# Quartered scores with full tables in the first two batches of a fused sliding-window attention and feed-forward kernel

## Chip, cores and metric

The kernel runs on one core of a Trainium2 chip. The metric is device microseconds of that core for one execution. A core has five engines with a queue of instructions each, worked off in order: TensorE (PE; weight loads are shown apart as PEld), VectorE (DVE), ScalarE (ACT), GpSimd (POOL) and SyncE (SP). [...] SyncE, ScalarE and GpSimd issue DMAs.

## The reference

Attention with a sliding window of 128 positions and a linear bias per head, then a feed-forward layer with a hard swish. The input is float32; the kernel computes in bf16 with float32 sums.

```python
B, H, S, D = 8, 8, 576, 64           # q, k, v: (B, H, S, D)
scores = q @ k.T / sqrt(D)
rel = pos[:, None] - pos[None, :]     # query position - key position
slopes = 2.0 ** (-8.0 * (arange(H) + 1) / H)
scores = where((rel >= 0) & (rel < 128), scores - slopes * abs(rel), -1e9)
x = softmax(scores) @ v               # -> (B*S, H*D) = (4608, 512)
h = x @ w_in                          # (4608, 2048)
out = (h * clip(h + 3, 0, 6) / 6) @ w_out   # (4608, 512), float32
```

## The kernel before

**Attention.** The work is cut into 32 pairs of heads, `g = 4 * batch + hp`, each with 576 positions in four key tiles of 128 and one of 64. Scores stand transposed in PSUM, keys on partitions and queries along the columns. A key tile j meets two blocks of queries: its own ("diagonal", rel from 0) and the next ("off", rel up to 127). Two PSUM buffers `score[0]` and `score[1]`, each of two banks (one bank per head of the pair), are handed out in turn by `score_banks()`.

Mask and bias reach the scores in two ways. In batches 2 to 7, `scores` works on quarters of TensorE's array (64 x 64: head e selects the rows, half of the key tile the columns), the exponential (`exp_diag`, `exp_off`) takes the bias as a column per partition (`bias_d`, `bias_o`), and GpSimd masks the result with `affine_select`. In batch 0 a table (`tab`, slopes times rel, with -2^30 where masked) is added in PSUM first: `tables_diag` and `tables_off` multiply it by the identity, `scores_diag` and `scores_off` add the products of k and q with 64 x 128 of the array, and one exponential of 1024 columns follows for each block. In batch 1 the off block has a table and the diagonal has bias columns and GpSimd's masks. `attend` (a whole pair in a score buffer), `attend_split` and `values` (in parts of three and two query tiles, in banks "av", "o" or "h") multiply by v, which has a column of ones, and VectorE divides by that column's result. `back` transposes a pair's result into `xT`, the input of the feed-forward part: by TensorE up to batch 1 and for two pairs of batch 2, by a transposing DMA afterwards.

**Loading.** q and k of batches 0 to 3 (k) or 2 (q) arrive as float32 in `ldbuf`, are cast to bf16 (`prepare`, `prepare_double`, `prepare_halves`) and transposed by TensorE: `transposes` for one pair on quarters of the array, `double...` and `wide...` for two pairs at once on the whole array. v is cast by `cast_v` or `cast_tokens`. The first 512 columns of w_in come as float32 through SyncE (`load_raw`, `cast_raw`), the rest of w_in and w_out through casting DMAs that GpSimd issues (`load_w_in`, `load_w_out`). Until w_out is loaded, `w_out_sb` holds the exponentials of batch 0 (`rooms`); those of batch 1 stand in `gbuf[1]`.

**Feed-forward.** Nine tiles of 512 tokens. `moe_up(nt, ms)` makes one of 16 column tiles: four matmuls of 512 columns into a PSUM bank, a ReLU on ScalarE (scaled by 1/6, bias 0.5), and on VectorE min with 1 times h into `gbuf`. `moe_down` does four of the 16 matmuls of an output tile per step. The up tiles use the two banks "h" in turn; `UP_BANKS` sends some of tile 0 to "av" and "o". `units` is the fixed list of these steps, and `fill(n)` takes the next n of them where their input exists (`done`).

**Order.** Everything is under a manual schedule: each engine's instructions stand in the order in which the Python calls them. `first_batch()` and `second_batch()` are written out by hand, with `fill` between the steps of attention; from pair 8 on `segment` does the same in a loop. `memset(ldbuf[2][:, 0:1])` near the end of `second_batch` (L768) is a fence: v of batch 2 is loaded into that buffer only after GpSimd has come to it. `warm_up(n)` runs n matmuls whose result nobody reads.

Of the kernel before, what the change touches and what calls it, by code (L numbers as in the profile page):

```python
# [10 lines left out]
FP32 = mybir.dt.float32  # L11
# [7 lines left out]
def kernel(  # L19
# [39 lines left out]
    tab = perm.tile([128, H, 2, 128], BF16)  # L59
# [63 lines left out]

    def constants():
        make_identity(nc, ident)
        nc.vector.memset(bias3, 0.5)
        nc.vector.memset(warm, 0.0)
        nc.scalar.activation(out=warm, in_=warm, func=ACT.Exp)
        nc.gpsimd.iota(rel_i, pattern=[[0, 1]], base=0, channel_multiplier=1)
        base = rpool.tile([128, NT], FP32, tag="r6", name="base")  # L130
        base_i = base[:, 0:256].bitcast(INT32).rearrange("p (s c) -> p s c", s=2)
        base_b = base[:, 256:384].bitcast(BF16).rearrange("p (s c) -> p s c", s=2)
        nc.gpsimd.iota(base_i, pattern=[[128, 2], [0, 128]], base=-192, channel_multiplier=1)
        nc.gpsimd.tensor_copy(out=base_b, in_=base_i)
        biases()
        nc.gpsimd.affine_select(out=base_b[:, 1, :], in_=base_b[:, 1, :], pattern=[[1, 128]],
                                channel_multiplier=-1, base=0,
                                compare_op=ALU.is_ge, fill=-(2.0 ** 30))
        nc.gpsimd.affine_select(out=base_b[:, 0, :], in_=base_b[:, 0, :], pattern=[[-1, 128]],
                                channel_multiplier=1, base=-1,  # L140
                                compare_op=ALU.is_ge, fill=-(2.0 ** 30))
        nc.vector.memset(kTb[0][:, :, 4, LAST:128], 0.0)
        for h in range(H):
            nc.vector.tensor_scalar(out=tab[:, h, :, :], in0=base_b, scalar1=slopes[h] / scale,
                                    scalar2=0.0, op0=ALU.mult, op1=ALU.add)
# [5 lines left out]
    def memsets_later():  # L151
        for i in range(2):
            nc.gpsimd.memset(p4buf[i], 1.0)
        nc.gpsimd.memset(kTb[1][:, :, 4, LAST:128], 0.0)
        nc.gpsimd.memset(vbuf[1][:, :, :, D:W], 1.0)
        nc.gpsimd.memset(vbuf[1][64:128, 4, :, 0:D], 0.0)
        nc.gpsimd.memset(tbuf[64:128, :, 4, :], 0.0)
# [7 lines left out]
    def biases():  # L165
        nc.vector.tensor_copy(out=rel_f, in_=rel_i)
        for h in range(H):
            nc.vector.tensor_scalar(out=bias_o[:, h:h + 1], in0=rel_f, scalar1=-192.0,
                                    scalar2=slopes[h], op0=ALU.add, op1=ALU.mult)

        for h in range(H):
            nc.vector.tensor_scalar(out=bias_d[:, h:h + 1], in0=rel_f, scalar1=-64.0,
                                    scalar2=slopes[h], op0=ALU.add, op1=ALU.mult)
# [20 lines left out]
    def second_w_in():  # L194
        nc.gpsimd.memset(w_out_sb[:, 4, 0:1], 0.0)
# [34 lines left out]
    def transposes(g, copies):  # L230
        b, hp = divmod(g, NP)
        for nm, dst, copy in (("q", qTb[b % 2], copies[0]), ("k", kTb[b % 2], copies[1])):
            src = st.pop((g, nm))
            tp = ps_h.tile([128, RT, RP], BF16, tag="h", name="tp", padded_shape=[128, 16, 64])
            for t in range(RT):
                for e in range(2):
                    r = slice(e * D, (e + 1) * D)
                    nc.tensor.transpose(tp[r, t, :], src[r, ts(t, D)], ident[r, r])  # L238
            copy(out=dst[:, hp, :, :].rearrange("p j c -> p (j c)")[:, 0:S].rearrange(
                "p (a t) -> p a t", t=RT), in_=tp.rearrange("p t a -> p a t"))  # L240
# [72 lines left out]
    def diag_tabled(g):  # L313
        return g < NP

    def tables_diag(g):
        scd = score_banks()
        st[g, "scd"] = scd
        for e in range(2 if diag_tabled(g) else 0):
            t = tab[:, 2 * (g % NP) + e, 1:2, :]  # L320
            nc.tensor.matmul(scd[:, e, :].rearrange("p (j c) -> p j c", j=4), lhsT=ident,
                             rhs=t.to_broadcast([128, 4, 128]), start=True, stop=False)

    def rooms(g):
        b, hp = divmod(g, NP)
        if full(g):
            room = w_out_sb if b == 0 else gbuf[1]
            for i, nm in enumerate(("pd", "po")):
                st[g, nm] = room[:, ds(4 * hp + 2 * i, 2), :].rearrange(
                    "p e (j c) -> p e j c", j=4)  # L330
        else:
            st[g, "pd"] = ppool.tile([128, 2, 4, 128], BF16, tag="pd", name="pd")
            st[g, "po"] = ppool.tile([128, 2, 4, 128], BF16, tag="po", name="po")

    def scores_diag(g):
        rooms(g)
        b, hp = divmod(g, NP)
        qT, kT = qTb[b % 2][:, hp, :, :], kTb[b % 2][:, hp, :, :]
        first = not diag_tabled(g)
        if (g, "scd") not in st:  # L340
            tables_diag(g)
        scd = st[g, "scd"]
        for j in range(4):
            for e in range(2):
                r = slice(e * D, (e + 1) * D)
                nc.tensor.matmul(scd[:, e, ts(j, 128)], lhsT=kT[r, j, :],  # L346
# [540 lines left out]
```

## Time and profile before

| | |
|---|---|
| timed runs | 320.58, 319.79, 320.45 us; median 320.45 us |
| profiled execution | span 317.9 us from first to last instruction; the profile lists no other time of it |
| instructions in it | 6980 |
| busy | PE 307.0 us, PEld 163.4, DVE 176.1, ACT 196.8, POOL 138.9 |
| granted TensorE clock | 1.000 of full |
| DMA | 52.43 MB, mean 165 GB/s |

A busy PE is not PE at its peak: matmuls are pipelined, and each row's duration holds some 0.17 us in which the next is already running. The distance between starts tells the rate. Rows of the timeline merge equal instructions (x4 is four of them) and give in brackets how long the engine was idle before, and what ended that.

### The profile page before, as it was taken

Reading aid. Unit: us, or ns where it says so; the run is one execution under the profiler, and the core shown is the slowest. Engines: PE = TensorE matmul, PEld = TensorE weight load, DVE = VectorE, ACT = ScalarE, POOL = GpSimd, SP = SyncE. Lnnn points to the kernel's source line nnn. Section 1 sums busy time; section 2 is a strip of 40 time slices with the busy share of each in tenths; the row PEclk is TensorE's granted clock in tenths of the full one; section 3 lists DMA queues with packets and bytes.
Section 4 is the critical chain, followed back from the end, with each engine's and each line's share of the span. In section 5 each row is a group of like instructions: output and inputs, shape, how many; then the busy total and the mean of one; then the engine's idle time right before and its main releaser. Section 6 shows DMA issues by size and latency. Waiting matters only on the chain.

```text
span 317.9 us, 6980 instructions
## 1 busy us (share of the span) xinstructions
PE 307.0 (97%) x2671; PEld 163.4 (51%) x2710; DVE 176.1 (55%) x344; ACT 196.8 (62%) x338; POOL 138.9 (44%) x247
## 2 busy tenths in 40 slices
PE   8889999999999999999999999999999999999996
PEld 3565474455554445555676644454444444444443
DVE  6677676554456654566465546564656455455510
ACT  3869986877767666766667756675764244244401
POOL 7358192674594684548463854472231000000000
PEclk9999999999999999999999999999999999999999
DMA  7999999999999999999999999934112100000112
GB/s 271 264 373 215 255 236 200 236 235 198 216 265 180 222 215 212 213 196 253 186 178 219 190 206 198 228 95 57 49 29 75 66 34 33 35 33 33 66 57 77
DMA packets 131425, 52.43 MB, mean 165 GB/s; under 512 B 118976, under 2 KB 122816, under 8 KB 131392
## 3 DMA queue, kind: packets, MB, share of 16 engines
q1 hardware_dynamic: 125648, 46.15, 69.0%
q0 software_dynamic: 3696, 3.67, 7.1%
q10 hardware_dynamic: 2048, 2.16, 2.2%
q8 instruction: 21, 0.34, 0.5%
q14 instruction: 12, 0.10, 0.1%
HBM read 36.70 MB, written 9.44 MB: 145 GB/s over the span
## 4 chain that ended last, share of the span: by engine, by line
PE 90%; ACT 3%; DVE 3%; issue 2%; POOL 0%; DVEq 0%; POOLq 0%; ACTq 0%
PE hps L532 38%; PE ops L587 37%; PE score L399 3%; PE av L463 2%; PE av L455 2%; DVE avs L485 1%; PE ops L568 1%; PE w L163 1%; ACT w_out_sb L422 1%; PE score L346 1%; PE tp L269 1%; ACT r L556 1%; DVE gbuf L557 1%; PE score L301 1%; PE score L357 1%
## 5 line engine op out<-in xcount | busy, mean ns | idle before, releaser
L556 ACT ACTIVATE r<-hps,bias 128x512 f32<-128x512 f32 x144 | 98.9, 689 | 84.2 <-PE hps L532 83.9
L557 DVE SCALAR_TENSOR_TENSOR gbuf<-r,hps 128x512 bf16<-128x512 f32 x144 | 98.8, 688 | 91.6 <-ACT r L556 90.1
L532 PE MATMUL hps<-xT,w_in_sb 128*128 128x512 bf16 (+1 forms) x623 | 142.0, 358 | 1.7 <-ACT xT L519 0.3
L587 PE MATMUL ops<-w_out_sb,gbuf 128*128 128x512 bf16 x538 | 133.8, 379 | 2.3 <-issue 1.8
L532 PEld LDWEIGHTS <-w_in_sb 128*128 128x128 bf16 x640 | 59.2, 98 | 54.0 <-issue 1.5
L587 PEld LDWEIGHTS <-gbuf 128*128 128x128 bf16 x560 | 52.4, 98 | 57.5
L427 POOL TENSOR_SCALAR_AFFINE_SELECT pd<-pd 128x512 bf16<-128x512 bf16 x48 | 29.4, 631 | 35.2 <-ACT pd L425 35.2
L436 POOL TENSOR_SCALAR_AFFINE_SELECT po<-po 128x512 bf16<-128x512 bf16 x48 | 30.1, 633 | 30.8 <-ACT po L434 30.1
L596 DVE COPY osb<-ops 128x512 f32<-128x512 f32 x33 | 22.7, 688 | 23.8 <-PE ops L587 23.7
L425 ACT ACTIVATE pd<-score,bias_d 128x512 bf16<-128x512 f32 x48 | 31.1, 683 | 6.4 <-PE score L399 6.4
L434 ACT ACTIVATE po<-score,bias_o 128x512 bf16<-128x512 f32 x48 | 33.1, 690 | 0.0
L213 POOL CAST tbuf<-ldbuf 128x512 bf16<-128x512 f32 (+1 forms) x45 | 25.7, 611 | 15.7 <-issue 14.6
L474 DVE TENSOR_TENSOR avs<-av,rc 128x384 bf16<-128x384 f32 (+1 forms) x48 | 23.6, 491 | 1.6
L463 PEld LDWEIGHTS <-pd 128*128 128x128 bf16 x192 | 14.3, 97 | 8.2 <-issue 0.2
L455 PE MATMUL av<-vbuf,po 128*128 128x65 bf16 x192 | 18.0, 193 | 0.0
L206 POOL CAST vbuf<-ldbuf 128x1024 bf16<-128x1024 f32 x14 | 14.3, 1041 | 7.6 <-DMA ldbuf<-in_v_dram 7.6
L463 PE MATMUL av<-vbuf,pd 128*128 128x65 bf16 x192 | 17.3, 194 | 0.0
L455 PEld LDWEIGHTS <-po 128*128 128x128 bf16 x192 | 14.3, 98 | 3.0 <-DVE avs L474 0.5
L439 ACT ACTIVATE p4buf<-score,bias_d 128x64 bf16<-128x64 f32 x48 | 15.6, 324 | 0.0
L399 PEld LDWEIGHTS <-kTb 64*64 64x64 bf16 x480 | 9.4, 106 | 9.1 <-issue 8.5
L399 PE MATMUL score<-qTb,kTb 64*64 64x192 bf16 (+1 forms) x480 | 13.1, 234 | 0.0
L246 POOL CAST pr<-ldbuf 128x576 bf16<-128x576 f32 x18 | 11.5, 668 | 2.6 <-PE tp L238 1.3
(107 smaller groups left out, 201.7 us busy)
## 6 DMA issues: line engine op xcount, KB each, us to landing
out_dram<-osb SPq DMA_DIRECT2D x33, 256.0 KB, 3.5
ldbuf<-in_v_dram SPq DMA_DIRECT2D x31, 256.0 KB, 4.6
ldbuf<-in_q_dram SPq DMA_DIRECT2D x20, 256.0 KB, 5.0
ldbuf<-in_k_dram SPq DMA_DIRECT2D x16, 256.0 KB, 5.3
ldbuf<-in_q_dram SPq DMA_DIRECT2D x12, 288.0 KB, 6.6
ldbuf<-in_k_dram SPq DMA_DIRECT2D x12, 288.0 KB, 6.7
w_out_sb<-in_moe_w_out_dram POOLq DMA_DIRECT2D x4, 512.0 KB, 9.1
w_in_sb<-in_moe_w_in_dram POOLq DMA_DIRECT2D x3, 512.0 KB, 8.8
```

What stands on the lines that cost most here:

```text
L213: nc.gpsimd.tensor_copy(out=tbuf[:m, :, j, :], in_=s[:m, j, :, :].rearrange("p (i e) d -> p i (e d)", e=2))
L399: nc.tensor.matmul(wide[e][c, ds(at, n)], lhsT=kT[r, j, c], rhs=qT[r, ds(q0, n)], start=True, stop=True)
L425: nc.scalar.activation(out=pd[:, e, :, :], in_=block_scores(g, e, False), func=ACT.Exp, bias=bias_d[:, h:h + 1], scale=scale)
L427: nc.gpsimd.affine_select(out=pd[:, e, :, :], in_=pd[:, e, :, :], pattern=[[0, 4], [1, 128]], channel_multiplier=-1, base=0, compare_op=AL ...
L434: nc.scalar.activation(out=po[:, e, :, :], in_=sc, func=ACT.Exp, bias=bias_o[:, h:h + 1], scale=scale)
L436: nc.gpsimd.affine_select(out=po[:, e, :, :], in_=po[:, e, :, :], pattern=[[0, 4], [-1, 128]], channel_multiplier=1, base=-1, compare_op=A ...
L455: nc.tensor.matmul(out_av, lhsT=po[:, e, (qt if full(g) else qt - 1) % 4, :], rhs=vb[:, qt - 1, h, :], start=True, stop=False)
L463: nc.tensor.matmul(out_av, lhsT=d, rhs=vb[:, qt, h, :], start=(qt == 0), stop=True)
L532: nc.tensor.matmul(hps[:, lo:hi], lhsT=w_in_sb[:, ks, ts(ms, 128)], rhs=xT[:, ks, ds(src, hi - lo)], start=(ks == 0), stop=(ks == n_ks - 1))
L556: nc.scalar.activation(out=r6, in_=hps, func=ACT.Relu, bias=bias3[:, 0:1], scale=1.0 / 6.0)
L557: nc.vector.scalar_tensor_tensor(out=gts[nt][:, ms, :], in0=r6, scalar=1.0, in1=hps, op0=ALU.min, op1=ALU.mult)
L587: nc.tensor.matmul(ops[nt, sub], lhsT=gts[nt][:, ms, ts(sub, 128)], rhs=w_out_sb[:, ms, :], start=(ms == 0), stop=(ms == n_ms - 1))
```

## The change

Batches 0 and 1 get one way of scoring. `tab` is laid out per pair and for both heads of it on two halves of the partitions, three steps of 64 positions deep, with the slope as a column (`slope2`); `slope_table` makes it per pair. A pair is scored in two halves t = 0, 1 of two key tiles each, both on quarters of the array: `tables(g, t)` first, with four matmuls of 512 columns for t = 0 and twelve of 256, 192 and 64 for t = 1, then `scores_full(g, t)` with eight or ten, and one exponential of 1024 columns for each half. No score of these batches is masked by GpSimd any more.

In batch 0 every pair is loaded and transposed alone, q and k of a pair one pair ahead of its scores, and all four pairs are attended in two parts (`attend_part`) in four banks, two of the second parts normalised by ScalarE. The first column tiles come after all four ways back, and three of the eight warm-up matmuls go. In batch 1 the halves alternate with single units; the first two pairs are attended with `attend_split`, the q and k of batch 2 are transposed in four parts whose copies all stand on ScalarE, and 16 units instead of 18 are called ahead of pair 8's scores. The bias columns for batches 2 to 7 are made by GpSimd in batch 1, behind the cast of v. The hard swish is kept times six (ReLU of h + 3, min with 6) and the output copies divide by six; two ReLUs of tile 0 go to VectorE.

```diff
+    def tables(g, t):
+        hp = g % NP
+        sc = st[g, "sc", t] = score_banks()
+        for c in range(2):
+            o = slice(c * 64, (c + 1) * 64)
+            for e in range(2):
+                r = slice(e * D, (e + 1) * D)
+                src = tab[r, hp, c + 1 - e, :]
+                row = sc[o, e, :]
+                if t == 0:
+                    nc.tensor.matmul(row.rearrange("p (j c) -> p j c", j=2), lhsT=ident[r, r],
+                                     rhs=src.rearrange("p (j c) -> p j c", j=1).to_broadcast(
+                                         [64, 2, 256]), start=True, stop=False)
+                    continue
+                for at, n in ((0, 256), (256, 192), (448, 64)):
+                    nc.tensor.matmul(row[:, ds(at, n)], lhsT=ident[r, r], rhs=src[:, 0:n],
+                                     start=(at == 0), stop=False)
+
+    def scores_full(g, t):
...
+        for j in (2 * t, 2 * t + 1):
+            for c in range(2):
+                q0 = j * 128 + c * 64
+                n = min(192, S - q0)
+                for e in range(2):
+                    r = slice(e * D, (e + 1) * D)
+                    nc.tensor.matmul(sc[ds(c * 64, 64), e, ds(j % 2 * 256 + c * 64, n)],
+                                     lhsT=kT[r, j, ds(c * 64, 64)], rhs=qT[r, ds(q0, n)],
...
-    UP_BANKS = {6: "o", 8: "av", 11: "o", 12: "av", 15: "o"}
+    UP_BANKS = {3: 'o', 8: 'o'}
...
-        nc.scalar.activation(out=r6, in_=hps, func=ACT.Relu, bias=bias3[:, 0:1], scale=1.0 / 6.0)
-        nc.vector.scalar_tensor_tensor(out=gts[nt][:, ms, :], in0=r6, scalar=1.0, in1=hps,
+        if nt == 0 and ms in BY_DVE:
+            nc.vector.tensor_scalar(out=r6, in0=hps, scalar1=3.0, scalar2=0.0, op0=ALU.add,
+                                    op1=ALU.max)
+        else:
+            nc.scalar.activation(out=r6, in_=hps, func=ACT.Relu, bias=bias3[:, 0:1], scale=1.0)
+        nc.vector.scalar_tensor_tensor(out=gts[nt][:, ms, :], in0=r6, scalar=6.0, in1=hps,
...
     def first_batch():
...
+        warm_up(5)
+        tables(0, 0)
+        tables(0, 1)
+        transpose_run(0, "q", V, "h")
+        transpose_run(0, "k", A, "h")
+        transpose_run(1, "q", V, "av")
+        scores_full(0, 0)
+        exp_full(0, 0)
+        transpose_run(1, "k", V, "o")
+        scores_full(0, 1)
+        exp_full(0, 1)
...
+        attend_part(0, 0, "h")
+        attend_part(1, 0, "h")
+        attend_part(2, 0, "av")
+        attend_part(3, 0, "o")
...
+        attend_part(0, 1, "h", A)
+        attend_part(1, 1, "h")
+        attend_part(2, 1, "av", A)
+        attend_part(3, 1, "o")
...
+        back(1, "h")
+        back(0, "h")
+        back(2, "av")
+        cast_raw(2, A)
+        back(3, "o")
+        cast_raw(3, V)
...
     def second_batch():
+        def part(i, t):
+            scores_full(NP + i, t)
+            exp_full(NP + i, t)
+        memsets_later()
+        part(0, 0)
+        fill(1)
+        part(0, 1)
...
+        part(1, 1)
+        cast_tokens(1, "v")
+        biases(nc.gpsimd)
         fill(2)
...
+        fill(1)
+        attend_split(NP, ("av", "o"))
+        part(3, 1)
+        fill(1)
+        back(NP, "av")
+        attend_split(NP + 1, ("o", "h"))
...
+        fill(1)
         attend(NP + 2)
         back(NP + 1, "av")
         attend(NP + 3)
+        fill(1)
+        double(2, 0, "k", 0, "h", A)
         back(NP + 2, "o")
+        double(2, 0, "k", 1, "av", A)
+        double(2, 0, "q", 0, "h", A)
+        back(2 * NP - 1, "o")
+        double(2, 0, "q", 1, "av", A)
         done[0] = 2 * NP
+        fill(1)
         scores(2 * NP)
+        fill(1)
```

377 lines of the change are left out of this document (150 added, 227 removed).

## The prediction

> **What bounds the kernel now.** I read the page first (busy shares, the chain that ended last), then the busy time by stage, then the timeline of the first 65 us engine by engine. The first fence has lines of the page (span, busy shares, shares of the chain) and two rows of the busy time by stage (start:end, length, then busy us of PE, PEld, DVE, ACT, POOL).
>
> ```profile
> span 317.9 us, 6980 instructions
> ...
> PE 307.0 (97%) x2671; PEld 163.4 (51%) x2710; DVE 176.1 (55%) x344; ACT 196.8 (62%) x338; POOL 138.9 (44%) x247
> ...
> PE 90%; ACT 3%; DVE 3%; issue 2%; POOL 0%; DVEq 0%; POOLq 0%; ACTq 0%
> ...
> 24.30:49.66 25.36, 24.53 (x276) 14.34 (x281) 19.32 (x30) 23.03 (x35) 16.93 (x27) 1.00 1.13 231
> ...
> 80.00:140.00 60.00, 58.75 (x537) 30.04 (x544) 33.16 (x68) 41.38 (x78) 38.24 (x68) 1.00 1.08 212
> ```
>
> TensorE carries 90% of the chain and is about full from the second batch on (24.53 of 25.36 us, later 58.75 of 60). From pair 8 on (the first of batch 2) the program is practically the same before and after. So the change is worth what it does to the moment when the scores of pair 8 start, corrected for the feed-forward work done by then. All 1152 matmuls of the feed-forward part have to run somewhere; a "unit" below is four of them, one column tile of the up projection.
>
> Timeline rows now (start, length, engine, line, and in brackets the idle time before and its releaser).
>
> ```profile
> 38.39 1.04 POOL L206 CAST vbuf<-ldbuf 128x1024 bf16<-128x1024 f32 x1 [6.60 <-DMA ldbuf<-in_v_dram]
> 39.50 0.61 POOL L209 CAST vbuf<-ldbuf 64x512 bf16<-64x512 f32 x1
> ...
> 40.36 0.23 PE L463 MATMUL score<-vbuf,gbuf 128*128 128x65 bf16 x2
> 40.91 1.03 PE L532 MATMUL hps<-xT,w_in_sb 128*128 128x512 bf16 x4
> ...
> 49.66 0.55 PE L399 MATMUL score<-qTb,kTb 64*64 64x192 bf16 x20
> 50.14 1.04 PE L587 MATMUL ops<-w_out_sb,gbuf 128*128 128x512 bf16 x4
> ```
>
> Two fixed points. The first attention of batch 1 starts at 40.36, right behind the last cast of v of batch 1 (39.50 + 0.61 = 40.11), and that cast waited for its DMA (6.60 us idle). The scores of pair 8 start at 49.66. Before, 18 units stand ahead of pair 8 in the program's order; after, 16. Ahead of the first attention of batch 1 stand 13 before and 12 after. So whatever batch 0 gains ahead of 40.1 us is lost again at the wait for v, unless v comes earlier: the bytes queued ahead of it are the same, and I keep 40.1.
>
> **The price of scores and tables.** Rows of table and score blocks, one early one at the half rate:
>
> ```profile
> 1.43 2.31 PE L163 MATMUL w<-ident 128*128 128x512 bf16 x5 [1.43 <-POOL ident masks.py:199]
> ...
> 15.69 0.33 PE L357 MATMUL score<-tab,ident 128*128 128x384 bf16 x1
> 15.85 0.22 PE L360 MATMUL score<-tab,ident 128*128 128x128 bf16 x1
> ...
> 28.14 0.40 PE L346 MATMUL score<-qTb,kTb 64*128 64x128 bf16 x8
> 28.47 0.45 PE L269 MATMUL tp<-ident,pr 128*128 128x128 bf16 x5
> 28.86 0.32 PE L357 MATMUL score<-tab,ident 128*128 128x384 bf16 x1
> ...
> 29.72 0.40 PE L269 MATMUL tp<-ident,pr 128*128 128x128 bf16 x4
> ```
>
> Before, a pair of batch 1 costs TensorE 0.33 us (28.14 to 28.47, diagonal) and 0.86 us (28.86 to 29.72, tables and off-diagonal): 1.19. After, a pair has two halves. Half 0: four table matmuls of 512 columns on four different quarters of the array, which overlap, about 0.27 us; eight score matmuls at 0.024 (20 take 0.48, 49.66 to 50.14) 0.20; entering and leaving the quartered mode some 0.07 each (the eight of L346 take 0.33 where eight at 29 ns would take 0.23): 0.61. Half 1: twelve table matmuls of 256, 192 and 64 columns, three in a row on the same quarter. Nothing in the trace has neighbours on one quarter. The bounds: overlapped as in L399, 0.30 us; or one behind the other as on the whole array (384 columns take 0.16, 15.69 to 15.85, 0.42 ns a column), where only the last of three overlaps the next quarter's first: 3 x 448 + 512 = 1856 columns, 0.78 us. I take 0.78, since all rows here begin in program order and L357 to L360 is the nearest pair. With ten score matmuls and the mode change half 1 is 1.17, a pair 1.78.
>
> [...]
>
> **Batch 0.** Rows of the exponentials and of what must stand between them and the first unit:
>
> ```profile
> 8.01 1.02 ACT L422 ACTIVATE w_out_sb<-score 128x1024 bf16<-128x1024 f32 x1 [0.78 <-PE score L346]
> ...
> 15.52 1.02 ACT L422 ACTIVATE w_out_sb<-score 128x1024 bf16<-128x1024 f32 x1
> 16.44 1.02 ACT L409 ACTIVATE w_out_sb<-score 128x1024 bf16<-128x1024 f32 x1
> 18.87 1.14 ACT L187 CAST w_in_sb<-gbuf 128x512 bf16<-128x512 f32 x2 [1.41 <-DMA gbuf<-in_moe_w_in_dram]
> 19.92 1.29 ACT L519 COPY xT<-tb 128x576 bf16<-128x576 bf16 x2
> ...
> 23.36 1.03 PE L532 MATMUL hps<-xT,w_in_sb 128*128 128x512 bf16 x4
> ...
> 58.34 0.32 ACT L439 ACTIVATE p4buf<-score,bias_d 128x64 bf16<-128x64 f32 x1
> 58.54 0.70 ACT L556 ACTIVATE r<-hps,bias 128x512 f32<-128x512 f32 x1
> ...
> 63.81 0.18 DVE L473 RECIPROCAL rc<-av 128x6 f32<-128x6 f32 x1
> 64.02 0.56 DVE L474 TENSOR_TENSOR avs<-av,rc 128x384 bf16<-128x384 f32 x1
> ```
>
> Both have eight exponentials of 1024, 0.92 apart (15.52 to 16.44); before they end at 17.46. After, ScalarE has no copies between them. The first comes at about 8.2 (three warm-up matmuls go, but half 1's tables run at the early half rate, 0.43 per 512 columns at 1.43 us). At each of three half 1's the freed bank needs 0.78 + 0.25 + 0.25 (latency) against 0.92: 0.39 lost. The last ends at 8.2 + 7 x 0.92 + 3 x 0.39 + 1.02 = 16.8. VectorE normalises the four first parts at 0.72 (16.3 to 19.2), then ScalarE does eight scalings of 64 columns at 0.24 (between 0.20, the distance 58.34 to 58.54, and 0.32): 21.3; two copies to xT (1.29) 22.6; the cast of the third slice of weights (0.57) 23.2. Only then the first unit's third matmul. Before, the first unit's last matmuls run at 23.36, with a second unit and the transposes of q and k beside them.
>
> **From there to the first attention of batch 1.** The unit takes 0.86; the transposes 0.50 per nine, 0.28 per five, 0.29 for a pair's way back:
>
> ```profile
> 59.17 0.86 PE hps L532 x4
> ...
> 46.19 0.45 PE L517 MATMUL tb<-ident,avs 128*128 128x128 bf16 x5 [0.34 <-DVE avs L485]
> 46.48 0.67 PE L301 MATMUL score<-ident,pr 128*128 128x128 bf16 x9
> 46.98 2.75 PE L532 MATMUL hps<-xT,w_in_sb 128*128 128x512 bf16 x11
> ```
>
> Twelve units less the two matmuls already done 9.9; q and k transposed twice, 1.0 + 1.0; four half 0's 2.4; three half 1's 3.5: 17.9, so 41.1, a little behind the wait for v (40.1).
>
> **From the first attention to pair 8.** Four units 3.45, the last half 1 1.17, four attentions at 0.55 (40.36 to 40.91) 2.2, four ways back 1.15, transposes of batch 2 1.0: 9.0. Waits on top, from these rows:
>
> ```profile
> 45.30 0.82 DVE L485 TENSOR_TENSOR avs<-score,rcw 128x640 bf16<-128x640 f32 x1
> ...
> 48.04 0.69 ACT L556 ACTIVATE r<-hps,bias 128x512 f32<-128x512 f32 x1 [0.19 <-PE hps L532]
> 48.87 1.51 DVE L557 SCALAR_TENSOR_TENSOR gbuf<-r,hps 128x512 bf16<-128x512 f32 x2
> ...
> 52.66 0.74 ACT L271 COPY kTb<-tp 128x640 bf16<-128x640 bf16 x1
> ```
>
> A unit's bank is free 0.19 + 0.69 + 0.69 = 1.6 us after its last matmul, later when VectorE is busy with a normalisation (0.82). The up-tiles now alternate over two banks, which the split attention and the transposes of batch 2 share: the fourteenth unit waits 0.4; the first q transposes, 0.8 us of TensorE work behind the fifteenth unit, wait 1.0 (VectorE still has pair 7's normalisation). All four copies of k and q (0.74 each) now stand on ScalarE beside a copy to xT: 0.5 before the last transposes and the scores. The way back of pair 4 waits 0.4 for the split normalisation, that of pair 6 0.2. Together 2.5; TensorE has nothing else in its order, so none is covered. Pair 8 starts at 41.1 + 9.0 + 2.5 = 52.6, 2.9 behind; two units (1.7) are still owed: **4.6 us**. On the span 317.9 + 4.6 = 322.5; the median of the runs shown, 320.45, lies 2.55 above the span, so **325.1**.
>
> **Costed at nothing.** The multiply by six moves a factor from the ReLU into output copies of the same size, and two ReLUs of tile 0 go to VectorE: both engines have room. The masks of batch 1 on GpSimd go; it stood idle 6.60 us for v anyway. The bias columns move to GpSimd, behind that cast and ahead of the issues of w_out, the casts for batch 2 and the fence (L768) that lets v of batch 2 start:
>
> ```profile
> 49.06 0.10 POOL L768 MEMSET ldbuf<- 128x1 f32 x1
> ...
> 62.36 0.61 POOL L209 CAST vbuf<-ldbuf 64x512 bf16<-64x512 f32 x1
> 62.69 0.23 PE L463 MATMUL av<-vbuf,pd 128*128 128x65 bf16 x2
> ```
>
> Seventeen small ones and two more casts against four masks put the fence 0 to 1.2 us later. Its reader came 13.0 us behind pair 8's scores (62.69) and now comes one unit later still, near 66.5; v would be there by 64. If the cover were gone, up to 1.2 us.
>
> **Rivals.** *The quarters overlap freely* (0.30): batch 0 ends 1.5 us earlier, the wait for v takes over at 40.1, the rest 8.5 + 2.5: pair 8 at 51.1, 1.4 + 1.7 = 3.1 late, 323.5. Against it: no such neighbours in the trace. *The other side:* v of batch 1 lands by 36, the quarters overlap and the banks never wait: first unit 21.6, 16.4 of work to 38.0, 8.5 more to 46.5: 3.2 earlier, less 1.7 owed, 1.5 faster, 319.0. It decides only if the cast at 38.39 moves forward by over 2 us; DMA has no spare share (1.13). With v at 40.1 and no wait at all it is still 0.7 slower. *Cold start:* without the extra warm-up, with small matmuls only, TensorE stays at the half rate through batch 0: each half 1 costs 0.8 more three times, 328. For it: the 0.43 rows; against: the tables at 15.69 run at the full rate in a batch 0 that is no denser.
>
> **Numbers.** Serial quarters 0.50, free overlap 0.27, cold start 0.10, no change 0.04, the faster case 0.09. A measurement of this kernel tells 0.3% (about 1 us) from no change. The range takes in the overlap case with half its waits (322) and most of the cold case: 321.5 to 327.
>
> **What would show it.** Right: the tables of half 1 take 0.7 to 0.8 us from first to last; first unit complete near 23.5; first attention of batch 1 at 41 to 42; scores of pair 8 near 52.6 with 16 units done; waits on the up-tile banks ahead of the transposes of batch 2. Wrong: pair 8 before 48, v of batch 1 cast before 38, or a different pace behind 65 us.

## The result and the profile after

| | before | after |
|---|---|---|
| median of the timed runs | 320.14 us (319.79 to 320.58) | 324.66 us (323.80 to 324.92) |
| ratio, 95% interval | | 1.0129 (1.0105 to 1.0153) |
| profiled execution | span 317.9 us | 324.7 us, span 323.0 us |
| scores of pair 8 start at | 49.66 us | 51.12 us |
| scores of pair 14 start at | 96.04 us | 101.09 us |

The change makes the kernel 4.5 us slower by the medians (4.1 by the ratio); 325.1 was forecast, in a range of 321.5 to 327.0. The path to that number was not the forecast one, as the rows show.

The page of the kernel after, the lines that answer to those shown of before:

```profile
span 323.0 us, 7250 instructions
...
PE 306.5 (95%) x2810; PEld 164.5 (51%) x2849; DVE 174.4 (54%) x337; ACT 196.2 (61%) x337; POOL 139.8 (43%) x260
...
PE 88%; ACT 3%; DVE 3%; issue 2%; DMA 1%; POOL 0%; SPq 0%; DVEq 0%; POOLq 0%
```

TensorE is busy for as long as before (306.5 against 307.0 us) in a span that is 5.1 us longer: the loss is waiting, not work. Next the timeline of the kernel after, TensorE's rows at the places that the prediction named.

```profile
23.40 1.04 PE L526 MATMUL hps<-xT,w_in_sb 128*128 128x512 bf16 x2 [0.29 <-ACT w_in_sb L192]
...
28.50 1.04 PE L526 MATMUL hps<-xT,w_in_sb 128*128 128x512 bf16 x4
29.46 0.42 PE L337 MATMUL score<-tab,ident 64*64 64x256 bf16 x11
29.71 0.25 PE L353 MATMUL score<-qTb,kTb 64*64 64x192 bf16 x1
...
30.01 0.68 PE L273 MATMUL tp<-ident,pr 128*128 128x128 bf16 x9
...
40.34 0.23 PE L434 MATMUL av<-vbuf,gbuf 128*128 128x65 bf16 x2
...
48.74 0.44 PE L273 MATMUL tp<-ident,pr 128*128 128x128 bf16 x5 [0.50 <-ACT kTb L275]
...
49.88 0.38 PE L273 MATMUL tp<-ident,pr 128*128 128x128 bf16 x4 [0.18 <-ACT kTb L275]
...
51.12 0.55 PE L383 MATMUL score<-qTb,kTb 64*64 64x192 bf16 x20
...
63.63 1.03 PE L526 MATMUL hps<-xT,w_in_sb 128*128 128x512 bf16 x3
64.49 0.39 PE L273 MATMUL tp<-ident,pr 128*128 128x128 bf16 x4
66.15 1.02 PE L526 MATMUL hps<-xT,w_in_sb 128*128 128x512 bf16 x4 [1.27 <-DVE gbuf L555]
...
101.09 0.55 PE L383 MATMUL score<-qTb,kTb 64*64 64x192 bf16 x20
```

Four things stand here. The tables of a second half take 0.25 us (29.46 to 29.71), not 0.78, and such a half costs 0.55 in all (29.46 to 30.01). The first attention of batch 1 starts at 40.34, pair 8 at 51.12. The waits for ScalarE's copies ahead of the last transposes are there. And behind pair 8, where the prediction had an unchanged pace, a unit waits 1.27 us for its bank at 66.15. From pair 14 on both kernels run alike, 5.05 us apart. The first fence below has rows of before, the place that answers to 66.15 and the scores of pair 14; the waits of TensorE for the product of a unit between 48 and 90 us follow (what waited, for what: us in total, times, longest), before and after.

```profile
61.60 0.39 PE L269 MATMUL tp<-ident,pr 128*128 128x128 bf16 x4
61.82 1.03 PE L587 MATMUL ops<-w_out_sb,gbuf 128*128 128x512 bf16 x4
...
63.33 1.02 PE L532 MATMUL hps<-xT,w_in_sb 128*128 128x512 bf16 x4 [0.17 <-DVE gbuf L557]
...
96.04 0.55 PE L399 MATMUL score<-qTb,kTb 64*64 64x192 bf16 x20
```

```profile
PE hps L532 <- DVE gbuf L557: 0.2, 1, 0.2
```

```profile
PE hps L526 <- DVE gbuf L555: 2.0, 3, 1.3
```

GpSimd's rows in the timeline of the kernel after:

```profile
38.53 1.05 POOL L210 CAST vbuf<-ldbuf 128x1024 bf16<-128x1024 f32 x1 [0.88 <-DMA ldbuf<-in_v_dram]
39.52 0.61 POOL L213 CAST vbuf<-ldbuf 64x512 bf16<-64x512 f32 x1
...
40.35 1.65 POOL L177 TENSOR_SCALAR bias_o<-rel_f 128x1 f32<-128x1 f32 x8
41.95 1.68 POOL L177 TENSOR_SCALAR bias_d<-rel_f 128x1 f32<-128x1 f32 x8
...
51.41 0.10 POOL L776 MEMSET ldbuf<- 128x1 f32 x1
...
64.98 0.61 POOL L213 CAST vbuf<-ldbuf 64x512 bf16<-64x512 f32 x1 [0.36 <-DMA ldbuf<-in_v_dram]
```

v of batch 1 is ready at 40.13, as before (40.11). With the column that they are made from (40.07), the bias columns take 3.5 us, so the fence comes 2.35 us later than before (51.41 against 49.06), where 0 to 1.2 was forecast.

### The profile page after: what moved, and what is told of

The parts are those of the page before. It is cut to its first block, busy times and chain, and to the rows that moved or that the text cites. A ratio compares the mean times of both kernels' runs of the same rounds, so it can differ in the third digit from the quotient of the medians.

```text
span 323.0 us, 7250 instructions
## 1 busy us (share of the span) xinstructions
PE 306.5 (95%) x2810; PEld 164.5 (51%) x2849; DVE 174.4 (54%) x337; ACT 196.2 (61%) x337; POOL 139.8 (43%) x260
## 4 chain that ended last, share of the span: by engine, by line
PE 88%; ACT 3%; DVE 3%; issue 2%; DMA 1%; POOL 0%; SPq 0%; DVEq 0%; POOLq 0%
PE hps L526 38%; PE ops L594 36%; PE score L383 3%; PE av L434 3%; PE av L432 2%; DMA ldbuf<-in_q_dram 1%; ACT r L554 1%; PE tp L273 1%; PE ops L575 1%; DVE gbuf L555 1%; PE tp L241 1%; PE score L353 1%; DVE tbuf L490 1%; ACT xT L513 1%; PE score L337 1%
## 5 line engine op out<-in xcount | busy, mean ns | idle before, releaser
L555 DVE SCALAR_TENSOR_TENSOR gbuf<-r,hps 128x512 bf16<-128x512 f32 x144 | 98.9, 687 | 97.8 <-ACT r L554 96.7
L554 ACT ACTIVATE r<-hps,bias 128x512 f32<-128x512 f32 x142 | 97.8, 689 | 87.2 <-PE hps L526 86.7
L564 DVE TENSOR_SCALAR osb<-ops 128x512 f32<-128x512 f32 (+1 forms) x34 | 23.0, 675 | 31.8 <-PE ops L594 25.6
```

The source lines that it names most:

```text
L554: nc.scalar.activation(out=r6, in_=hps, func=ACT.Relu, bias=bias3[:, 0:1], scale=1.0)
L555: nc.vector.scalar_tensor_tensor(out=gts[nt][:, ms, :], in0=r6, scalar=6.0, in1=hps, op0=ALU.min, op1=ALU.mult)
```

## Experiments

All times are medians; each ratio is against runs of the kernel before on the same chip, taken beside those of the row. These had medians of 319.8 to 320.3 us.

| kernel | time, us | ratio to before (95%) | pair 8 | pair 14 |
|---|---|---|---|---|
| after | 324.66 | 1.0129 (1.0105 to 1.0153) | 51.12 | 101.09 |
| 18 units ahead of pair 8 | 323.12 | 1.0086 (1.0061 to 1.0111) | 53.37 | 99.61 |
| bias columns early | 324.41 | 1.0123 (1.0079 to 1.0166) | 51.12 | 101.09 |
| extra matmuls in batch 0 | 324.51 | 1.0125 (1.0082 to 1.0169) | 51.25 | 101.22 |
| wide transposes of batch 2 | 324.25 | 1.0116 (1.0073 to 1.0159) | 50.92 | 100.75 |
| second w_in slice early | 324.81 | 1.0130 (1.0102 to 1.0159) | 51.49 | 101.47 |
| old second half of batch 1 | 321.12 | 1.0025 (1.0007 to 1.0044) | 50.98 | 97.23 |
| rotated tables (one run) | 324.25 | | 50.68 | 100.67 |
| 18 units and wide transposes | 322.60 | 1.0094 (1.0076 to 1.0112) | 52.34 | 98.58 |
| 18 units and whole attentions | 322.99 | 1.0101 (1.0085 to 1.0117) | 53.33 | 99.56 |
| before, hard swish times six | 320.05 | 0.9988 (0.9972 to 1.0004) | 50.08 | 96.47 |
| quarter scores in the old order | 320.64 | 1.0010 (0.9994 to 1.0027) | 50.15 | 96.39 |
| the same, unit 13 earlier | 320.66 | 1.0007 (0.9995 to 1.0019) | 50.09 | 96.34 |

The last two columns are the starts of those pairs' scores in the profiled execution. Pair 14 is the place to compare, since by then all these kernels have done the same work.

**The order of units.**

```diff
         done[0] = 2 * NP
-        fill(1)
+        fill(3)
         scores(2 * NP)
-        fill(1)
```

> The changed kernel with eighteen up-projection units ahead of the scores of pair 8 in place of sixteen and none behind them, so that from pair 8 on the interleaving of units and pairs is the one of the kernel before; the total work is the same. Theory A (the order of units that lags by one puts neighbouring up-tiles on the two banks while VectorE copies transposes, which shows as 0.41 + 0.27 + 1.27 us of waits of TensorE for the product of L555 between 57 and 66 us): these waits go, about 1.9 us shorter than the changed kernel, 322.8. Theory B (the loss behind pair 8 comes from late data, the fence or v of batch 2, not from the order): no change, 324.7 within 0.4.

Measured: 323.12, 1.5 us less than after (1.4 by the ratios), and pair 14 1.48 us earlier. No wait for the product of L555 is left between pair 8 and 90 us; a new one of 0.64 us stands ahead of unit 17, since units 15, 16 and 17 now share two banks. Timeline of this kernel:

```profile
28.30 1.04 PE L526 MATMUL hps<-xT,w_in_sb 128*128 128x512 bf16 x4 [0.73 <-DMA w_in_sb<-in_moe_w_in_dram]
...
52.41 1.02 PE L526 MATMUL hps<-xT,w_in_sb 128*128 128x512 bf16 x4 [0.64 <-DVE gbuf L555]
53.37 0.55 PE L383 MATMUL score<-qTb,kTb 64*64 64x192 bf16 x20
...
99.61 0.55 PE L383 MATMUL score<-qTb,kTb 64*64 64x192 bf16 x20
```

Theory A holds, with 0.4 us less than it gave, and with the new wait ahead of unit 17 beside it. In the changed kernel the list of units runs one behind the pairs. At 66.15 this shows: the second part of the transposes (64.49) holds one of the two banks "h", so the next up tile gets the bank that the unit just ahead (63.63) has filled, and waits for that unit's ReLU and product. In the kernel before, a step of the down projection stands between the two (61.82), and the wait was 0.17 us.

**The bias columns** ahead of the cast of v:

```diff
+        biases(nc.gpsimd)
         cast_tokens(1, "v")
-        biases(nc.gpsimd)
```

> The changed kernel with the bias columns made on GpSimd ahead of the cast of v of batch 1, where GpSimd stands idle 5.7 us, in place of behind it. The fence that lets v of batch 2 start comes about 3.4 us earlier (near 48 us in place of 51.4). Theory A (the fence is hidden: v of batch 2 is cast by 65.6 and read at 67.0): no change, within 0.3 us of the changed kernel. Theory B (late casts on GpSimd hold up the transposes of batch 2 and the chain behind them): 1 to 2 us shorter.

Measured: 324.41. The fence comes at 48.43 in place of 51.41, and TensorE's rows stay where they were (pair 14 at 101.09 in both). Theory A: the later fence is hidden, as the prediction said, though it was twice as late as its bound.

**The clock.** The granted clock of the kernel after is recorded as low for 3.4 us. Busy time by stage, three rows of after (start:end, length, busy us of PE, PEld, DVE, ACT and POOL with their counts, granted clock, DMA share, GB/s):

```profile
21.00:22.00 1.00, 1.00 (x13) 0.95 (x10) 0.86 (x3) 0.80 (x3) 1.00 (x2) 0.50 1.14 301
22.00:23.00 1.00, 1.00 (x8) 0.63 (x6) 0.28 (x1) 1.00 (x3) 0.72 (x2) 0.50 1.15 298
23.00:24.00 1.00, 0.71 (x3) 0.36 (x3) 0.51 (x2) 0.91 (x2) 0.17 (x1) 0.50 1.13 286
```

So the ways back and the first unit ran at half rate. The test puts work into the gaps ahead of it:

```diff
         load_tokens(1, "v")
+        st["warm"] = score_banks()
+        score_banks()
+        keep_warm(1)
         attend_part(0, 1, "h", A)
+        keep_warm(1)
         attend_part(1, 1, "h")
+        keep_warm(1)
         attend_part(2, 1, "av", A)
+        keep_warm(3)
         attend_part(3, 1, "o")
```

> The changed kernel with six extra matmuls of 512 columns, whose result is not read, set into the idle time of TensorE between 17.6 and 20.4 us (one, one, one, three, ahead of the four second parts of the attention of batch 0). Theory A (the sparse stretch lets the granted clock fall to 0.50 from 21 to 24.4 us, which makes the way back of batch 0 take 2.07 in place of 1.05 us and the first unit late): the clock stays at 1.00 there and the kernel gains 0.7 to 1.0 us. Theory B (the wait for v of batch 1 at 40.1 us takes all of it): the clock stays up, the first attention of batch 1 stays at 40.1 to 40.3, gain at most 0.2 us. Theory C (the gap does not set the clock): clock still 0.50 there, no gain or a loss of up to 0.5.

Measured: 324.51, first attention of batch 1 at 40.46, just outside the 40.1 to 40.3 of theory B. The clock was 1.00 from 20 to 24 us, but half between about 13 and 19; in the profile of the kernel with the wide transposes, whose batch 0 is that of the kernel after, it was half between 8 and 12. Busy time by stage, first of the kernel with the extra matmuls, then of that with the wide transposes:

```profile
16.00:18.00 2.00, 2.00 (x48) 1.83 (x41) 0.58 (x2) 1.56 (x2) 1.34 (x3) 0.50 1.03 383
```

```profile
8.00:10.00 2.00, 1.67 (x58) 1.31 (x54) 1.52 (x3) 1.83 (x2) 1.53 (x3) 0.56 1.24 270
...
22.00:24.00 2.00, 1.25 (x14) 0.73 (x13) 0.79 (x2) 1.87 (x4) 0.70 (x2) 1.00 1.16 296
```

So the place of the slow stretch changes between executions of the same batch 0: from 21 us also in the profile with early bias columns, from 8 us also in that with 18 units, from 16 us in that with the old second half, and in those of the rotated tables and of the two parts tried on 18 units there is none. One profile can't say what set it, and whether the gaps did, as theory A has it, stays open.

The column of the clock is not the whole record. It shows 1.00 ahead of the first change that was recorded, where the distances between starts show half rate. Timeline of the kernel after:

```profile
9.06 0.63 PE L332 MATMUL score<-tab,ident 64*64 64x512 bf16 x2
...
9.21 0.62 PE L332 MATMUL score<-tab,ident 64*64 64x512 bf16 x2
9.49 0.66 PE L353 MATMUL score<-qTb,kTb 64*64 64x192 bf16 x8
...
11.28 0.41 PE L332 MATMUL score<-tab,ident 64*64 64x512 bf16 x4
11.49 0.36 PE L353 MATMUL score<-qTb,kTb 64*64 64x192 bf16 x8
```

Four such tables take 0.43 us at 9.06 and 0.21 at 11.28. In the kernel before, two tables on the whole array took 1.06 us at 3.53 and 0.59 at 9.08: it was at the full rate by then, so the kernel after came to it later.

What all this costs can be bounded: in the profiles of the kernel after and of the seven others with the same work ahead of the first attention of batch 1 (18 units and the two parts tried on it, bias columns, extra matmuls, wide transposes, rotated tables) this attention starts between 39.79 and 40.46, wherever the clock was low. Part of what batch 0 gains is lost on the way there, but not by a wait for v: no idle time of TensorE stands ahead of the attention in any of them. Where batch 0 ends early, TensorE mostly waits at unit 4 for the second slice of w_in (0.73 us at 28.30 in the kernel with 18 units); where the clock was halved late, unit 4 comes at 28.50 and waits for nothing.

**That slice, loaded earlier:**

```diff
+        second_w_in()
         cast_v(0, 0, P)
...
             nc.gpsimd.memset(p4buf[i], 1.0)
-        second_w_in()
```

> The changed kernel with the load of the second slice of w_in issued on GpSimd ahead of the five casts of v of batch 0 (near 12.4 us) in place of behind them (16.64 us). In the runs of the changed kernel whose first unit was early, unit 4, the first that reads this slice, stood waiting for its transfer (0.73 and 0.65 us, start 28.3 and 28.5 us), and in the one whose clock was halved between 21 and 24 us unit 4 came at 28.5 without waiting. Theory A (this transfer, and v of batch 1 right behind it at 40.1 us, both hold TensorE; whichever is moved, the other stays): unit 4 up to 1 us earlier, first attention of batch 1 still at 40.0 to 40.3, kernel within 0.3 us of the changed one. Theory B (this transfer alone is the anchor): first attention near 39.4, 0.7 to 1.0 us shorter. Theory C (the transfers of batch 0 queue behind it): batch 0 ends later and the kernel is 0.3 to 1 us longer.

Measured: 324.81. A's time, by C's mechanism: the last cast of v of batch 0 starts at 18.27 in place of about 15.6, behind 2.61 us of waiting for its transfer, the first unit's third matmul comes at 24.23, and no wait for that slice is left. The clock was half from about 13 to 20 us in this profile, so that delay is not all the transfers'; that nothing is gained, the time shows. v of batch 1 is ready at 38.94 here, 1.2 us earlier, and the first attention starts at 40.71, 0.4 us later: v does not hold it.

**The transposes of batch 2:**

```diff
-        double(2, 0, "k", 0, "h", A)
         back(NP + 2, "o")
-        double(2, 0, "k", 1, "av", A)
-        double(2, 0, "q", 0, "h", A)
-        back(2 * NP - 1, "o")
-        double(2, 0, "q", 1, "av", A)
+        wide_double(2, 0, "k", A)
+        back(2 * NP - 1, "av")
+        wide_double(2, 0, "q", V)
```

> The changed kernel with k and q of batch 2 transposed as before the change: nine transposes into a score bank and one copy each, k on ScalarE, q on VectorE, in place of four part copies on ScalarE. Theory A (the four copies of 0.75 us on ScalarE, beside two copies to xT, hold up the last transposes, the unit and the scores of pair 8 by 0.50 + 0.18 us and the copies queue ahead of a ReLU): pair 8 starts 0.7 to 1.2 us earlier and the kernel is that much shorter. Theory B (the wide tile waits for the normalisation of pairs 6 and 7, which hold the score banks, so the wait only changes its name): within 0.4 us of the changed kernel.

Measured: 324.25; pair 14 0.34 us earlier. Theory B: instead of 0.50 + 0.18 us for ScalarE's copies TensorE waits 0.25 us for a normalisation and 0.59 us for the copy of q ahead of the scores.

**The old second half of batch 1 as a whole:**

```diff
-    UP_BANKS = {3: 'o', 8: 'o'}
+    UP_BANKS = {3: 'o', 8: 'o', 15: 'o'}
...
+        biases(nc.gpsimd)
         cast_tokens(1, "v")
-        biases(nc.gpsimd)
...
         part(3, 0)
         fill(1)
-        attend_split(NP, ("av", "o"))
         part(3, 1)
-        fill(1)
-        back(NP, "av")
-        attend_split(NP + 1, ("o", "h"))
+        up_begin(0, 12, n_ks, "av")
+        attend(NP)
+        fill(1)
...
-        fill(1)
+        up_begin(0, 13, n_ks)
+        attend(NP + 1)
+        back(NP, "o")
         attend(NP + 2)
+        up_begin(0, 14, n_ks)
         back(NP + 1, "av")
         attend(NP + 3)
-        fill(1)
-        double(2, 0, "k", 0, "h", A)
+        fill(2)
         back(NP + 2, "o")
-        double(2, 0, "k", 1, "av", A)
-        double(2, 0, "q", 0, "h", A)
-        back(2 * NP - 1, "o")
-        double(2, 0, "q", 1, "av", A)
+        wide_double(2, 0, "k", A)
+        back(2 * NP - 1, "av")
+        wide_double(2, 0, "q", V)
+        fill(1)
         done[0] = 2 * NP
-        fill(1)
+        fill(2)
         scores(2 * NP)
-        fill(1)
```

Unit 15 goes to bank "o", a third one beside the two "h".

> The changed kernel with the second half of batch 1 in the order of the kernel before: all scores of pair 7 and unit 12 (on the spare bank) ahead of the first attention, all four attentions whole and in score banks, units 13 and 14 begun between them, k and q of batch 2 transposed as wide tiles, units 15, 16 and 17 ahead of pair 8; the bias columns ahead of the cast of v, so that GpSimd has its casts ready. The quarter scores, batch 0 and the hard swish stay changed. Theory A (beyond the 1.6 us of the unit order, the new order behind the first attention loses another 2.3 us in waits of TensorE for copies and banks): first attention at 41.7, pair 8 with eighteen units at 51.0, time 320.8. Theory B (the whole attentions wait for the last exponentials and the score banks, as the split ones were there to avoid): pair 8 at 52.5 or later, time 322.5 to 323.1.

Measured: 321.12 (1.0025 of before). Its timeline:

```profile
41.68 0.23 PE L434 MATMUL score<-vbuf,gbuf 128*128 128x65 bf16 x2
...
47.50 0.45 PE L510 MATMUL tb<-ident,avs 128*128 128x128 bf16 x5 [0.34 <-DVE avs L456]
...
50.98 0.55 PE L383 MATMUL score<-qTb,kTb 64*64 64x192 bf16 x20
```

Theory A, within 0.02 us at both places; the time lies 0.3 us above it. The busy time of the stretch that holds six units, four attentions, the last second half of scores and the transposes of batch 2, in the kernel with 18 units and then in this one:

```profile
40.12:53.37 13.25, 11.40 (x156) 7.16 (x157) 9.65 (x21) 9.03 (x14) 10.81 (x31) 1.00 1.05 227
```

```profile
40.26:50.98 10.72, 10.27 (x155) 7.09 (x157) 9.54 (x18) 7.25 (x11) 7.68 (x13) 1.00 1.11 242
```

The same matmuls take 13.25 us in the one order and 10.72 in the other, 2.5 us less. TensorE idles for 1.85 and for 0.45 of them. The rest of the difference, 1.1 us, lies in the busy sums; that these grow because each break in the work adds the tail of the matmul ahead of it (some 0.17 us of a row) is a reading, not shown by itself.

**Two parts of that alone**, on the kernel with 18 units and early bias columns: the wide transposes, and the whole attentions at the places of the split ones.

```diff
-        double(2, 0, "k", 0, "h", A)
...
+        wide_double(2, 0, "k", A)
...
+        wide_double(2, 0, "q", V)
```

> The kernel with eighteen units ahead of pair 8 and the bias columns ahead of the cast of v, and of the old second half of batch 1 only its end: k and q of batch 2 as wide tiles (k copied on ScalarE, q on VectorE) in place of four part copies on ScalarE, with the three units of tiles 15 to 17 behind them; the two split attentions stay. This divides the 2.0 us between the kernel with eighteen units (323.1) and the one with the old second half (321.1). Theory A (the waits for ScalarE's copies, 0.49 + 0.18 us, and for the bank ahead of unit 17, 0.64 us, are most of it): 321.6 to 322.1, pair 8 near 52.1. Theory B (the split attentions and the single buffers they take are most of it): 322.6 to 323.0.

```diff
-        attend_split(NP, ("av", "o"))
+        attend(NP)
...
-        attend_split(NP + 1, ("o", "h"))
+        attend(NP + 1)
```

> The kernel with eighteen units ahead of pair 8 and the bias columns ahead of the cast of v, with the attentions of pairs 4 and 5 whole, in a score bank each, at the places of the split ones; the four part copies of k and q on ScalarE stay. Theory A (the copies and banks of the tail are most of the 2.0 us): 322.6 to 323.1. Theory B (the split attentions are most of it): 321.4 to 322.0.

Measured: 322.60 (1.0094) and 322.99 (1.0101), neither below the ratio of the kernel with 18 units (1.0086). The two expectations had each part give way to the other; both results say that neither carries the 2.0 us by itself. The profiles say the same: from the first attention to pair 8 the kernel with 18 units takes 13.25 us, with the wide transposes 12.55, with the whole attentions 13.03. In the first, TensorE still waits 0.69 us ahead of unit 17, in the second the ways back wait 0.43 us for the whole normalisation, and the 0.49, 0.19 and 0.63 us at the tail stay. What is left to the full order is the rest of the list above: unit 12 and the scores of pair 7 ahead of the first attention, the units between attentions begun without their ReLU, unit 15 on a third bank. Which of these matters was not tried alone.

**The hard swish times six on the kernel before:**

```diff
-        nc.scalar.activation(out=r6, in_=hps, func=ACT.Relu, bias=bias3[:, 0:1], scale=1.0 / 6.0)
...
+        nc.scalar.activation(out=r6, in_=hps, func=ACT.Relu, bias=bias3[:, 0:1], scale=1.0)
...
-                nc.vector.tensor_copy(out=osb, in_=ops[nt, sub])
+                sixth_v(out=osb, in_=ops[nt, sub])
```

> The kernel before with the hard swish times six alone (bias 3, minimum with 6, the division by six in the copies of the output), nothing else. Theory A (same operations of the same sizes on the same engines): no difference, within 0.3 us of 320.1. Theory B (a scaled copy of the output on VectorE or ScalarE is slower than the plain one and sits on the path at 36 places): 0.5 to 2 us longer.

Measured: 320.05, ratio 0.9988 (0.9972 to 1.0004). Theory A.

**The order of the twelve tables:**

```diff
-                for at, n in ((0, 256), (256, 192), (448, 64)):
...
+        for at, n in ((0, 256), (256, 192), (448, 64)) if t else ():
+            for c in range(2):
+                for e in range(2):
```

> The changed kernel with the twelve table matmuls of a second half issued so that neighbours go to different quarters of the array (256 columns to each of the four, then 192, then 64) in place of three in a row to one quarter. The sums per quarter are the same. Theory A (quarters run side by side whatever the order, as the 0.25 us of the changed kernel's trace suggests): 0.24 to 0.26 us from the first to the first score matmul, time as the changed kernel. Theory B (a queue of three on one quarter holds up the others in part, hidden in the 0.25): 0.20 us or less, kernel up to 0.6 us shorter over twelve halves.

Timeline of this kernel:

```profile
29.06 0.41 PE L340 MATMUL score<-tab,ident 64*64 64x256 bf16 x12
29.31 0.33 PE L356 MATMUL score<-qTb,kTb 64*64 64x192 bf16 x8
```

0.25 us again, time 324.25 in one run: theory A. 512 columns to each quarter take little more than 512 columns on the whole array (0.21 us at 0.42 ns, the prediction's figure), whether three in a row go to one quarter or neighbours to different ones. The single matmuls in the trace of the kernel after tell why the order is all one: the four tables of 256 columns start 10 ns apart at 29.46 us, the four of 192 at 29.60, the four of 64 at 29.68, though the program has all three of one quarter ahead of the next quarter's. That is the order in which the program of this kernel has them.

**All of the arithmetic, none of the order:** the kernel before with the change's tables, scores, exponentials and hard swish.

```diff
-        scores_diag(NP + 0)
-        exp_diag(NP + 0, 0)
-        exp_diag(NP + 0, 1)
+        scores_full(NP + 0, 0)
+        exp_full(NP + 0, 0)
         up_begin(0, 2, n_ks, "av")
-        scores_off(NP + 0)
-        exp_off_full(NP + 0)
+        scores_full(NP + 0, 1)
+        exp_full(NP + 0, 1)
```

> The quadrant tables, quarter scores, whole exponentials without masks and hard swish times six of the change, in the order of the kernel before throughout: its loads and transposes of batch 0 (pairs 2 and 3 as a double), whole attentions in score banks, its units, banks and copies in both batches, bias columns on VectorE at the start. So the re-ordering of batches 0 and 1 is undone and the arithmetic change kept. Theory A (the quarter scores are the cheaper form, 1.06 us of TensorE a pair against 1.19, and all of the loss is order): batch 1 saves 0.5 us, of which the wait for v of batch 1 at 40.1 takes back some; 319.6 to 320.1, the same as the kernel before or a little faster. Theory B (the 0.8 us that the kernel with the old second half of batch 1 is still behind come from the quarter scores themselves): 320.8 to 321.2.

Measured: 320.64, ratio 1.0010 (0.9994 to 1.0027). That lies between the two theories (A ends at about 1.000 of before, B begins at 1.002), and its interval reaches both; a gain that can be told is not there. The profiled execution comes to the first attention at 40.85 (before 40.36) and needs 55.54 us from there to pair 14 (before 55.68). The half microsecond that the scores save in batch 1 does not arrive; between two profiles of an unchanged batch 0 this start differs as much (40.36 before, 40.78 with the hard swish times six).

```diff
         up_begin(0, 12, n_ks, "av")
+        up_begin(0, 13, n_ks)
         attend(NP)
...
-        up_begin(0, 13, n_ks)
         attend(NP + 1)
```

> As the kernel with the quarter scores in the old order, and unit 13 moved ahead of the first attention of batch 1, to fill the wait for v of batch 1. Theory A (TensorE comes to the first attention before v is cast at 40.1 us and waits there): pair 8 up to 0.5 us earlier than without the move, 319.2 to 319.8. Theory B (no wait for v stands there): within 0.3 us of the kernel without the move, or later by a bank wait for unit 14.

Measured: 320.66 (1.0007, 0.9995 to 1.0019). Theory B: the unit went into no gap, and the first way back now waits 0.70 us for its normalisation. No kernel tried here is faster than the one before by what this measurement can tell.

## Why the prediction came out as it did

That the forecast of 325.1 and the measured 324.66 agree is luck: errors of like size cancel. Pair 8 came 1.5 us earlier than forecast, and the way from there to pair 14 took 1.9 us more than forecast.

- **Half 1 at 0.78 us: wrong, 0.25.** The step that failed is the choice between its bounds: rows of the whole array (L357 to L360) were taken as nearest, when the four tables of a first half had been costed as overlapping on different quarters. A second half costs 0.55 us in place of 1.17. Pair 8 came at 51.12, where the overlap rival had put it (51.1), and not at 52.6: 0.8 us of the difference lie ahead of the first attention (40.34, 41.1 forecast), 0.7 behind it. The prediction took rows that begin in program order for work done one behind the other, which the 0.25 us excludes, and by the starts at 29.46 to 29.71 the order itself doesn't hold between quarters here. The quarters worked side by side, three matmuls in a row on one quarter included: 512 columns on each of four in 0.25 us, where 512 on the whole array take 0.21 (at 384 in 0.16, 15.69 to 15.85 before). Entering and leaving the quartered mode, 0.07 us each in the sum, cost 0.06 together: 0.55 less 0.25 for the tables and 0.24 for ten scores.
- **First unit at 23.2: right in the sum (23.40), not in its terms, so by luck too.** By the overlap it should have come some 1.5 us earlier. But the last exponential ended at 17.25 (16.8 forecast), and the ways back ran at half clock. TensorE had stood idle for 1.64 us in the middle of the transposes of pair 3's k, until 13.68, and the profile shows nothing that it waited for. From 12 to 14 us TensorE was busy for 0.36 us there, and in the profiles with 18 units, early bias columns, extra matmuls and wide transposes for 0.85, 0.45, 0.57 and 0.87; the cause stays open. The cold-start rival came true in part: TensorE was at half rate until some time between 9.5 and 11.3 us, later than before, but not throughout batch 0, and the late half clock stands at one of four places, from 8, 13, 16 or 21 us, or is missing (three profiles). Two small sums are also off: 0.78 + 0.25 + 0.25 against 0.92 loses 0.36, not 0.39 (the 0.25 of latency was an estimate; in the kernel before tables start 0.05 us behind the exponential that frees their bank, 14.50 to 14.55, and an exponential 0.04 behind the row of its scores, 13.44 to 13.48), and eight scalings of 0.24 from 19.2 end at 21.1, not 21.3.
- **The wait for v at 40.1 as the anchor: right as a time, wrong as a cause.** No idle time stands ahead of that attention, before or after: a unit runs right up to it (in the kernel before one weight load waited 0.3 us for v, beside that unit), and with v ready at 38.94 (second slice of w_in early) it started at 40.71. What holds TensorE in part is unit 4, whose slice of w_in lands near 28 us: in the kernel with 18 units the first unit's third matmul came 0.54 us earlier (22.86), the attention 0.22.
- **From the first attention to pair 8: right in the sum.** 11.0 us by the overlap rival (8.5 + 2.5), measured 10.78. The waits for ScalarE's copies (0.50 and 0.18) are in their places; in all TensorE idled for 1.21 us, not 2.5, and was busy for 9.57, not 8.5. That this order costs 2.0 us against the old one was found by the old second half of batch 1.
- **"From pair 8 on practically the same", two units owed, 1.7 us: wrong, 3.6.** Pair 8 to pair 14 took 49.97 us (51.12 to 101.09) against 46.38 before: 1.7 for the two units and 1.9 for bank waits. The list of units is the same but stands one unit behind the pairs until pair 13, and that brings up tiles together where the other bank is taken. The prediction's own sign of an error, a different pace behind 65 us, is what the trace shows. Undoing the lag gave 1.5 us back.
- **From the span to the time: 2.55 us added, 1.7 in fact.** The median of the runs and the span of one faster execution were set side by side; in the profiled run of the kernel after, the time lies 1.7 us above the span (324.7 and 323.0).
- **Costed at nothing: right.** Early bias columns, with the earlier fence, and the hard swish times six moved nothing that can be told, each by a run. The two ReLUs on VectorE were not tried alone.

Of the 4.5 us, the unit order is 1.5 and the rest of the second half of batch 1 is 2.0, both shown by undoing them one on the other. What is left is 0.8 by the ratio (1.0025, interval 1.0007 to 1.0044): the order of batch 0 and of the first half of batch 1, and the quarter scores. The quarter scores with the rest of the arithmetic in the old order are within 0.9 us (1.0027) and not told from nothing; the intervals of the two kernels overlap, so how the 0.8 us divide stays open.

## What to carry to other kernels

Where a fixed list of fill-in work runs beside a loop with its own rhythm, moving one or two entries across the loop's start shifts every later meeting of the two: compare the alignment, not only the amount. With TensorE as the bound, cost a re-ordering by who holds each bank and which engine empties it; here the same matmuls took 10.7 or 13.3 us. A saving ahead of a transfer that lands at a fixed time is lost in part at the wait for it (0.54 us ahead of it were 0.22 behind it here), and an event right behind another has not yet waited for it: look for idle time between the two before one is taken as the anchor of a forecast.

## What the runs showed of the hardware

Twelve table matmuls on quarters of the array, 512 columns for each quarter, took 0.25 us in both orders. In the kernel after, those on different quarters started 10 ns apart, in another order than the program's.

The granted TensorE clock fell to 0.50 in batch 0 once in each of seven profiles and at four places: for 3.4 us from 21 us, from 8 or from 16, for 6.8 us from 13 (the lengths of all but the first worked out from the mean clock of their stages). In three profiles with the same batch 0 it did not fall. What sets it, no run here shows: in the kernel after TensorE was busy for 6.70 of the 10 us from 10 to 20, ahead of the fall at 21. Ahead of the first change that is recorded the profile's clock reads 1.00, while four tables took 0.43 us at 9.06, twice their 0.21 at 11.28.

Sixteen operations of one element per partition took GpSimd 0.2 us each (1.65 us for eight).
